# Scores of two heads as 64-row products on the halves of TensorE's array

## The chip, the cores and the metric

The kernel runs on one core of one Trainium2 chip. The metric is device time in microseconds (us) of one execution. Before the change the median of three runs is 859.24 us (858.61 to 861.03).

## What is computed

Attention with a block mask over 4 batches, 8 heads, 576 positions and head size 64, then two feed-forward layers over the 2304 tokens:

```python
scores = scale * np.matmul(q, k.transpose(0, 1, 3, 2))
mask = block_i >= block_j                 # blocks of 64 positions
scores = np.where(mask, scores, -1000000000.0)
attn = softmax(scores)
x = attn @ v                              # heads joined: 2304 x 512
h = np.maximum(np.maximum(x @ w1, x @ w2), x @ w3); y = h @ w_out
h = np.maximum(y @ w_in, 0.0);            out = h * h @ w_out2
```

Everything comes in as float32 (the feed-forward weights as 64-bit words). To keep that precision at speed, the kernel splits an operand into a rounded part ("hi", type fp32r) and what the rounding left ("lo"), and sums two or three fast products in place of one slow float32 product.

## The kernel before, in words

The work goes by **pairs** of heads: 16 pairs, four per batch. The first four pairs (n = 0 to 3, `S_F32` is 1) multiply float32 queries and keys directly; the other twelve (n = 4 to 15) use split operands made by `score_operands` (line 460 on). A pair has five steps, `step(0)` to `step(3)` with 128 queries each, and `last_step` with the 64 remaining queries of both heads side by side. Step i computes scores of 128 queries against N = 128(i+1) keys, head by head, into the PSUM banks `sc` (three buffers; steps 0 and 1 put both heads into one bank, as their widths fit). Then VectorE masks and takes the row maximum `nm`, ScalarE takes the exponential `P`, TensorE transposes `P` into `tp`, and after all steps `values` multiplies with the values into `av`. The value products use 64 columns of the array for each head; the last of them has only 64 rows as well.

For the scores of a split pair, `score_operands` loads for each head a tile `raw` in which queries and keys (64 features) stand twice, on partitions 0 to 63 and 64 to 127. The stationary tile `qs` holds the query's hi part in the upper half and its lo part in the lower, so that one 128-row product with the keys' hi part `kh` and one with the lo part `kl` give all four cross terms: two products a head. For `last_step` it loads keys and zero-padded queries once more (`kt`, `zt`) and splits them too (`k2`, `z2`).

While attention of batch b runs, the first feed-forward layer (`mlp1`) of an earlier batch fills TensorE: its products are called `l` in the profile. After attention (at about 375 us) come the rest of `mlp1` and then the second layer (`ph`, `acc`).

All compute instructions are recorded as operations and then issued by `Plan.issue`, which keeps a clock for each engine from the cost table in `duration` (line 316 on) and always issues the operation that could start first, the lower rank first among equals. So each engine's order is fixed in the program. Every operation is recorded at line 187. The engines and the DMA queue (SP) work through their lists in that order. TensorE's list alternates pieces of attention with `l` products.

Of the kernel before, what the change touches and what calls it, by code (L numbers as in the profile page):

```python
# [12 lines left out]
F32 = mybir.dt.float32  # L13
F32R = mybir.dt.float32r
I32 = mybir.dt.int32
U32 = mybir.dt.uint32
AF = mybir.ActivationFunctionType
ALU = mybir.AluOpType
# [5 lines left out]
B, H, S, D = 4, 8, 576, 64  # L24
# [13 lines left out]
TAIL = 512  # L38
# [3 lines left out]
SCALE = 0.125  # L42
PAIRS = B * NPAIR

CFG = dict(PD=-1, PE=1, A1=0, A2=0, WP=1, FC=(8, 16), WO=24, FI=0, LO2=0, HI2=0, Q2=0, RN=3, XL=2, HL=2, SO=0, TF=0, W_A=0.7, W_B=1.5, SPARE='hl..rhl..rhl..r..r..r', S=15, PB=3, QB=(2, 2, 3), BANKS=(3, 2, 1, 2), LO=0, HI=0, Q=0, EV=('*', '*'), EV2=('a', 'a'), CB=2, PC=0, PM=1000, PX=-0.5, PO=0, HH='*', XH='*', N0='a', YS='a', HIS=0, RB=1, TB=(2, 1), KB=1, CT='a', LT='d', XA=4, XB=0)
# [5 lines left out]
PB = CFG["PB"]  # L51
# [244 lines left out]
def width(x):  # L296
    return math.prod(x.area.shape[1:])
# [15 lines left out]
def duration(engine, op):  # L313
    views = op.views()
    n = max(map(width, views))
    psum = any(x.psum for x in views)
    if engine == "pe":
        stat, mov = op.args[1:] if op.args[1:] else (op.kw["lhsT"], op.kw["rhs"])
        if op.name == "transpose":
            return 109  # L320
        n, m = width(op.args[0]), width(stat)
        if stat.tile.args[1] == F32:
            return (4 * n / 2.4 + 5) * (0.5 if m == 64 else 1)
        return max(n, 230) / 2.4 + (11 if n < 300 else 13)
    if engine == "act":
        if op.name == "activation" and "accum_out" in op.kw:
            return 455 + 0.834 * n
        return (160 if psum else 200) + 0.82 * n
    if engine == "pool":
        return 140 + 2.25 * n  # L330
    if engine == "sp":
        return 60
    if op.name == "memset":
        return 60 + n
    if op.name == "reciprocal":
        return 150 + 6.4 * n
    if op.name in ("tensor_scalar", "tensor_copy", "copy") and not psum:
        return (200 if isinstance(op.kw.get("scalar1"), View) else 150) + n / 1.92
    return 157 + n / 0.96


def transfer(op):
    x = next(v for v in op.views())
    return 128 * 4 * width(x) / 320.0


@with_exitstack
def fused_kernel(ctx: ExitStack, tc: tile.TileContext, z0, k0, qk, v, w123, wo1, win2, wo2, out):
    nc = Plan(tc)
# [22 lines left out]
    def bank(name, tag):  # L372
        return ps.tile([128, 512], F32, tag=tag, bufs=BANKS[tag], name=name)
# [54 lines left out]
    def cp(e, **kw):  # L428
        return {"a": nc.scalar.copy, "d": nc.vector.tensor_copy, "*": nc.any.tensor_copy}[e](**kw)
# [22 lines left out]
    def small(name):  # L452
        return at.tile([128, 2], F32, tag=name[:2], bufs=6, name=name)
# [2 lines left out]

    def score_operands(n):


        score = []
        for h in range(2):
            raw = at.tile([128, 2, S], F32, tag="raw", bufs=CFG["RB"], name=f"raw{n}_{h}")
            nc.sync.dma_start(out=raw, in_=qk[n, :, h])
            qs, kh, kl = [at.tile([128, S], F32R, tag=t, bufs=m, name=f"{t}_{n}_{h}")
                          for t, m in zip(("qs", "kh", "kl"), CFG["QB"])]
            nc.scalar.activation(out=qs, in_=raw[:, 0], func=AF.Copy, scale=SCALE)
            nc.scalar.copy(out=kh, in_=raw[:, 1])
            nc.vector.scalar_tensor_tensor(out=qs[64:128], in0=raw[64:128, 0], scalar=SCALE,  # L470
                                           in1=qs[64:128].bitcast(F32), op0=ALU.mult, op1=ALU.subtract)
            nc.vector.tensor_tensor(out=kl, in0=raw[:, 1], in1=kh.bitcast(F32), op=ALU.subtract)
            score.append([(qs, kh), (qs, kl)])


        kt = at.tile([128, S], F32, tag="kraw", bufs=1 + CFG["TF"], name=f"kt{n}")
        zt = at.tile([128, 2, 64], F32, tag="zraw", bufs=1 + CFG["TF"], name=f"zt{n}")
        nc.sync.dma_start(out=kt, in_=k0[n])
        nc.sync.dma_start(out=zt, in_=z0[n, :, :, TAIL:])
        if CFG["TF"]:  # L480
            return score, [(zt.rearrange("p h q -> p (h q)"), kt)]
        k2 = [at.tile([128, S], F32R, tag=f"k2{x}", bufs=CFG["KB"], name=f"k2{x}_{n}") for x in "hl"]
        z2 = [at.tile([128, 2, 64], F32R, tag=f"z2{x}", bufs=CFG["KB"], name=f"z2{x}_{n}") for x in "hl"]
        for f, (hi, lo) in ((kt, k2), (zt, z2)):
            cp(CFG["CT"], out=hi, in_=f)
            (nc.gpsimd if CFG["LT"] == "p" else nc.vector).tensor_tensor(out=lo, in0=f, in1=hi.bitcast(F32), op=ALU.subtract)
        z2 = [z.rearrange("p h q -> p (h q)") for z in z2]
        return score, [(z2[1], k2[0]), (z2[0], k2[1]), (z2[0], k2[0])]

    def score_operands_f32(n, g):  # L490


        a, w = GROUPS[g] if n < NPAIR else (0, S)
        if n < NPAIR and g == 0:
            zk = at.tile([128, 3, GA], F32, tag="tb", bufs=2 * CFG["TB"][1], name=f"zk{n}")
            z, k = [zk[:, h] for h in range(2)], zk[:, 2]
        else:
            z = [at.tile([128, w], F32, tag=t, bufs=CFG["QB"][2 * (t == "kl")], name=f"z{n}_{t}") for t in ("qs", "kl")]
            k = at.tile([128, S], F32, tag="kh", bufs=CFG["QB"][1], name=f"k{n}")
        nc.sync.dma_start(out=z[0], in_=z0[n, :, 0, a:a + w])  # L500
        nc.sync.dma_start(out=k, in_=k0[n, :, :a + w])
        nc.sync.dma_start(out=z[1], in_=z0[n, :, 1, a:a + w])
        return [[(z[h], k)] for h in range(2)], None
# [25 lines left out]
    def attn_pair(n, groups=(0, 1)):  # L529
# [17 lines left out]
        def sc_tag(i):  # L547
            turn[0] += 1
            return "mlp" if (i < 2 and n < CFG["XA"] or i >= 2 and n < CFG["XB"]) and turn[0] % 5 in (1, 3) else "sc"
# [9 lines left out]
        def step(i):  # L559
# [1 line left out]
            name = f"{n}_{i}"  # L561

            share = i < 2
            sc = [bank(f"sc{name}_{h}", sc_tag(i)) for h in range(1 if share else 2)]
            P = [at.tile([128, 576], F32, tag="P", bufs=PB, name=f"P{name}_{h}") for h in range(len(sc))]
            if share:
                both = sc[0][:, :2 * N].rearrange("p (h k) -> p h k", h=2)
                sc = [both[:, h] for h in range(2)]
                P = [P[0][:, N * h:N * h + N] for h in range(2)]
            nm = small(f"nm{name}")  # L570
            scale = SCALE if sf else 1.0
            sm = sums[i // 2][:, 2 * (i % 2):2 * (i % 2) + 2] if direct else small(f"sm{name}")
            for h in range(2):
                for c, (qp, kp) in enumerate(score[h]):
                    mm(sc[h][:, :N], qp[:, 128 * i - q0:128 * i - q0 + 128], kp[:, :N], start=c == 0,
                       stop=c == len(score[h]) - 1)
                if not share:
                    nc.vector.memset(sc[h][0:64, N - 64:N], MASKED / scale)
                    nc.vector.tensor_reduce(out=nm[:, h:h + 1], in_=sc[h][:, :N], axis=AX.X, op=ALU.max, negate=True)
            if share:  # L580
                nc.vector.memset(both[0:64, :, N - 64:N], MASKED / scale)
                nc.vector.tensor_reduce(out=nm, in_=both, axis=AX.X, op=ALU.max, negate=True)
            if sf:
# [22 lines left out]
        def last_step():  # L606
# [3 lines left out]
            for x in range(2):  # L610
# [4 lines left out]
                else:  # L615
                    for c, (qp, kp) in enumerate(last):
                        mm(sc[x][:, :HALF], qp, kp[:, ks], start=c == 0, stop=c == len(last) - 1)
                nc.vector.tensor_reduce(out=nm[:, x:x + 1], in_=sc[x][:, :HALF], axis=AX.X, op=ALU.max, negate=True)
            nc.vector.tensor_scalar(out=nm[:, 0:1], in0=nm[:, 0:1], scalar1=nm[:, 1:2], scalar2=SCALE, op0=ALU.min,
                                    op1=ALU.mult)  # L620
            for x in range(2):
                act = nc.scalar.activation(out=P[:, HALF * x:HALF * x + HALF], in_=sc[x][:, :HALF], func=AF.Exp,
                                           bias=nm[:, 0:1], scale=SCALE, accum_out=sm[:, x:x + 1])
            nc.vector.tensor_scalar(out=sm[:, 0:1], in0=sm[:, 0:1], scalar1=sm[:, 1:2], scalar2=None, op0=ALU.add)
            if not direct:
                reciprocals(sm[:, 0:1])
# [40 lines left out]
                       ident[:, o:o + m], start=True, stop=True)  # L667
            return rows

        if 0 in groups:  # L670
            for i in range(2):
                step(i)
                yield
            values(0)
        if 1 in groups:
            for i in range(2, 4):
                step(i)
                yield
            last_step()
            yield  # L680
            values(1)

    def split_x(b, g):
        with nc.ranked(CFG["PX"]):
# [440 lines left out]
```

## Time and profile before

| what | value |
|---|---|
| median of three runs | 859.24 us |
| the profiled execution's own time | 860.5 us |
| its span, first to last instruction | 858.4 us |
| TensorE busy | 836.4 us, 97% of the span |
| VectorE busy | 641.3 us, 75% |
| ScalarE busy | 486.1 us, 57% |
| GpSimd busy | 131.0 us, 15% |
| moved by DMA | 190.32 MB |

The span is 2.1 us shorter than the execution's own time; the profiled execution is 1.3 us longer than the median. Matmuls are pipelined: a record of one lasts longer than the distance to the next one, so what a matmul costs TensorE is read from start to start in the timeline, not from its duration.

### The profile page before, as it was taken

The page shows a single profiled execution, that of the slowest core. Times are in us where ns is not written, and L with a number is a line of the kernel's source. Part 1 is how long each engine was busy: PE and PEld are TensorE (multiplying, and loading weights), DVE is VectorE, ACT ScalarE, POOL GpSimd, SP SyncE. Part 2 cuts the span into 40 slices and gives each one's busy share as a digit, 9 for nine tenths or more (in the row PEclk, how much of TensorE's full clock was granted, in tenths as well). Part 3 has the DMA queues.
Part 4 walks back from the last instruction along what each step waited for, and adds up shares of the span by engine and source line. Part 5 has one row for each costly group of instructions (what it writes and reads, how often), then busy time and mean ns, then how long its engine had stood idle before and what let it go on. Part 6 is the DMA issues. An engine that isn't in the chain of part 4 may idle for free.

```text
span 858.4 us, 15996 instructions
## 1 busy us (share of the span) xinstructions
PE 836.4 (97%) x5608; PEld 786.6 (92%) x5608; DVE 641.3 (75%) x1389; ACT 486.1 (57%) x1138; POOL 131.0 (15%) x126
## 2 busy tenths in 40 slices
PE   6899999999999999999999989999999999999998
PEld 4567799999899989999999989999999999999998
DVE  5998778888889888855667866688466876387663
ACT  6888778777787877756465332455232653133441
POOL 2334302122022011124445110000000000000000
PEclk9999999999999999999999999999999999999999
DMA  9554445465556446346787389898987878987782
GB/s 307 195 183 141 159 146 171 142 212 183 162 181 206 118 168 201 107 158 231 237 299 265 132 304 385 260 323 259 305 273 251 254 252 285 292 257 251 253 268 90
DMA packets 96575, 190.32 MB, mean 222 GB/s; under 512 B 13040, under 2 KB 23280, under 8 KB 96496
## 3 DMA queue, kind: packets, MB, share of 16 engines
q1 hardware_dynamic: 96496, 189.31, 66.4%
q8 instruction: 45, 0.74, 0.4%
q14 instruction: 34, 0.28, 0.1%
HBM read 150.47 MB, written 38.80 MB: 220 GB/s over the span
## 4 chain that ended last, share of the span: by engine, by line
PE 93%; DMA 3%; ACT 2%; DVE 2%; SPq 0%; issue 0%; ACTq 0%; DVEq 0%
PE l L187 35%; PE acc_x L187 12%; PE ph_x L187 11%; PE ph_z L187 8%; PE acc_z L187 6%; PE av L187 6%; PE sc L187 5%; PE tp L187 4%; PE acc_y L187 3%; PE sc_t L187 2%; DMA ws<-ws_d 1%; PE tp_t L187 1%; DMA raw<-in_qk 1%; DMA ws_d<-wst 1%; DMA zk<-in_k 1%; ACT P L187 0%
## 5 line engine op out<-in xcount | busy, mean ns | idle before, releaser
L187 PE MATMUL l<-xhl,w1h 128*128 128x320 f32 (+1 forms) x1152 | 244.8, 300 | 0.0
L187 PEld LDWEIGHTS l<-xhl,w1h 128*128 128x128 f32 x1152 | 188.4, 190 | 4.5 <-issue 2.9
L187 PE MATMUL l<-xhl,w1l 128*128 128x256 f32 (+1 forms) x576 | 175.0, 304 | 0.0
L187 PEld LDWEIGHTS l<-xhl,w1l 128*128 128x128 f32 x576 | 109.3, 190 | 3.4 <-issue 1.5
L187 PE MATMUL acc_x<-g_p,ws 128*128 128x384 f32 x576 | 102.2, 335 | 0.0
L187 PEld LDWEIGHTS acc_x<-g_p,ws 128*128 128x128 f32 x576 | 100.1, 188 | 0.0
L187 PE MATMUL l<-hh,wo 128*128 128x320 f32 (+1 forms) x384 | 81.6, 298 | 2.9 <-DVE wo L187 2.1
L187 PE MATMUL ph_x<-t,ws 128*128 128x384 f32 x432 | 80.8, 335 | 0.0
L187 PEld LDWEIGHTS ph_x<-t,ws 128*128 128x128 f32 x432 | 75.4, 188 | 0.0
L187 ACT ACTIVATE P<-sc,nm 128x128 f32<-128x128 f32 (+3 forms) x128 | 66.8, 532 | 9.5 <-DVE nm L187 7.0
L187 DVE TENSOR_TENSOR run<-l,run 128x256 f32<-128x256 f32 (+1 forms) x96 | 43.7, 455 | 32.2 <-PE l L187 30.6
L187 PEld LDWEIGHTS l<-hh,wo 128*128 128x128 f32 x384 | 63.3, 190 | 3.7 <-DVE wo L187 2.5
L187 ACT CAST g_p<-c_wo 128x768 fp32r<-128x768 f32 x42 | 35.1, 836 | 38.7 <-PE acc_x L187 15.7
L187 PE MATMUL l<-hl,wo 128*128 128x256 f32 (+1 forms) x192 | 57.0, 299 | 0.0
L187 PE MATMUL tp<-ident,P 128*128 128x128 f32 x320 | 52.9, 281 | 4.2 <-ACT P L187 3.9
L187 PE MATMUL ph_z<-b,ws 128*128 128x384 f32 x288 | 53.9, 336 | 2.9 <-DMA ws<-ws_d 2.9
L187 DVE TENSOR_TENSOR g_p<-c_wo,g_p 128x768 fp32r<-128x768 f32 x42 | 39.9, 955 | 22.0 <-ACT g_p L187 21.8
L187 DVE TENSOR_REDUCE nm<-sc 128x2 f32<-128x256 f32 (+2 forms) x96 | 54.6, 588 | 0.6
L187 POOL TENSOR_TENSOR f_wo<-f_wo,raw_wo 128x512 int32<-128x512 int32 x22 | 30.3, 1378 | 161.6 <-ACT t L187 34.7
L187 PEld LDWEIGHTS ph_z<-b,ws 128*128 128x128 f32 x288 | 50.2, 188 | 3.2 <-issue 3.2
L187 PE MATMUL acc_z<-g_p,ws 128*128 128x384 f32 x288 | 51.2, 335 | 0.0
L187 PEld LDWEIGHTS acc_z<-g_p,ws 128*128 128x128 f32 x288 | 50.1, 188 | 0.0
(168 smaller groups left out, 1653.1 us busy)
## 6 DMA issues: line engine op xcount, KB each, us to landing
ws<-ws_d SPq DMA_DIRECT2D x336, 256.0 KB, 3.9
ws_d<-wst SPq DMA_DIRECT2D x64, 256.0 KB, 3.4
raw<-in_qk SPq DMA_DIRECT2D x24, 576.0 KB, 3.8
ws_d<-wst SPq DMA_DIRECT2D x24, 512.0 KB, 5.9
raw_wo<-in_wo SPq DMA_DIRECT2D x22, 512.0 KB, 3.8
raw_w<-in_w SPq DMA_DIRECT2D x18, 512.0 KB, 5.0
raw_wi<-in_win SPq DMA_DIRECT2D x16, 512.0 KB, 5.2
v<-in_v SPq DMA_DIRECT2D x16, 320.0 KB, 3.4
```

Source lines behind the costliest of these rows:

```text
L187: return getattr(engine, op_name)(*map(value, args), **{k: value(x) for k, x in kw.items()})
```

## The change

Queries and keys are loaded once per pair, head 0 on partitions 0 to 63 and head 1 on 64 to 127, and rounded once: one tile `parts` with query hi, key hi, key lo, query lo. A score step makes three products a head, lo x hi, hi x lo and hi x hi, each of 64 rows: head 0 on the upper half of TensorE's rows, head 1 on the lower, each head into a bank of its own. The products alternate between the heads, and the first of each two is recorded as waiting for what the second waits for. `last_step` uses the same `parts` for the keys, and queries copied into a zero-padded tile `z2`, which is cleared once at the start. The copies `kt`, `zt`, `k2` are gone. Steps 0 and 1 of split pairs now mask and reduce each head apart. The float32 pairs keep their way of working (their tiles have moved into the tag `parts`). `duration` gets a cost for the new products, and so the written order changes on all engines.

```diff
@@ duration
+        if m == 128 and stat.area.shape[0] == 64:
+            return (4 * n if stat.tile.args[1] == F32 else max(n, 230)) / 4.8 + 6
@@ score_operands
+        raw = at.tile([128, 2, S], F32, tag="raw", bufs=CFG["RB"], name=f"raw{n}")
+        nc.sync.dma_start(out=raw, in_=qk[n])
+        parts = at.tile([128, 4, S], F32R, tag="parts", bufs=2, name=f"parts{n}")
+        qh, kh, kl, ql = [parts[:, i] for i in range(4)]
+        nc.scalar.copy(out=kh, in_=raw[:, 1])
+        nc.scalar.activation(out=qh, in_=raw[:, 0], func=AF.Copy, scale=SCALE)
+        nc.vector.tensor_tensor(out=kl, in0=raw[:, 1], in1=kh.bitcast(F32), op=ALU.subtract)
+        nc.vector.scalar_tensor_tensor(out=ql, in0=raw[:, 0], scalar=SCALE, in1=qh.bitcast(F32), op0=ALU.mult,
+                                       op1=ALU.subtract)
+        z = z2[n % 2]
         score = []
         for h in range(2):
-            raw = at.tile([128, 2, S], F32, tag="raw", bufs=CFG["RB"], name=f"raw{n}_{h}")
...
-            score.append([(qs, kh), (qs, kl)])
...
+            rows = slice(64 * h, 64 * h + 64)
+            score.append([(x[rows], y[rows]) for x, y in ((ql, kh), (qh, kl), (qh, kh))])
+            nc.vector.tensor_copy(out=z[rows, :, 64 * h:64 * h + 64], in_=parts[rows, 0:4:3, TAIL:])
+        return score, [(z[:, 1], kh), (z[:, 0], kl), (z[:, 0], kh)]
@@ step
+            if rows:
+                for c in range(len(score[0])):
+                    pair = [product(h, c) for h in range(2)]
+                    pair[0].deps |= pair[1].deps
```

**TensorE, step 0 of pair 7** (`sc` is the score bank, `l` a feed-forward product; `x2` counts equal rows, the last size is that of the output). Before, head 0's two products, with feed-forward products before and after:

```order
582 L187 MATMUL l_0_1_5_0_2201<-xhl_1_647,w1l_990 128x320
583 L187 MATMUL sc_0_0_2222<-kh_0_2099,qs_0_2144 128x128
584 L187 MATMUL sc_0_0_2222<-kl_0_2121,qs_0_2144 128x128
585 L187 MATMUL l_0_1_5_0_2201<-xhl_1_647,w1h_951 128x320 x2
586 L187 MATMUL l_0_1_5_0_2201<-xhl_1_647,w1l_990 128x320
```

Now, both heads' products in one stretch of six, again between feed-forward products:

```order
598 L187 MATMUL l_0_1_5_1_2210<-xhl_1_630,w1h_915 128x320 x2
599 L187 MATMUL sc_0_0_2225<-parts_1895 128x128
600 L187 MATMUL sc_0_1_2227<-parts_1895 128x128
601 L187 MATMUL sc_0_0_2225<-parts_1895 128x128
602 L187 MATMUL sc_0_1_2227<-parts_1895 128x128
603 L187 MATMUL sc_0_0_2225<-parts_1895 128x128
604 L187 MATMUL sc_0_1_2227<-parts_1895 128x128
605 L187 MATMUL l_0_1_5_1_2210<-xhl_1_630,w1l_937 128x320
```

A step's four products of 128 rows (sixteen a pair in its four steps) have become six of 64 rows (twenty-four a pair), and the six stand together between products of 128 rows.

**TensorE, step 3 of pair 7.** Before, the products of 512 keys:

```order
657 L187 MATMUL sc_3_0_2433<-kh_0_2099,qs_0_2144 128x512
658 L187 MATMUL tp_0_0_2438<-ident,P_0_0_2380 128x128 x2
659 L187 MATMUL sc_3_0_2433<-kl_0_2121,qs_0_2144 128x512
660 L187 MATMUL l_0_1_1_2388<-hh_1_1607,wo_1107 128x320
661 L187 MATMUL sc_3_1_2449<-kh_1_2291,qs_1_2269 128x512
662 L187 MATMUL sc_3_1_2449<-kl_1_2341,qs_1_2269 128x512
```

Now, behind value products (64 columns) and ahead of the last step (128 rows):

```order
683 L187 MATMUL av_0_2468<-ta_2420,v_0_2026 64x128 x2
684 L187 MATMUL sc_3_0_2474<-parts_1895 128x512
685 L187 MATMUL sc_3_1_2478<-parts_1895 128x512
686 L187 MATMUL sc_3_0_2474<-parts_1895 128x512
687 L187 MATMUL sc_3_1_2478<-parts_1895 128x512
688 L187 MATMUL sc_3_0_2474<-parts_1895 128x512
689 L187 MATMUL sc_3_1_2478<-parts_1895 128x512
690 L187 MATMUL sc_t_2488<-parts_1895,z_116 128x288 x3
```

Here one side of the stretch meets value products, so that only one of its borders is new against products of 128 rows and columns.

**ScalarE, the operands of pair 7.** Before, with other work between them, five long roundings (`qs`, `kh` for either head, `k2h`) and a short one (`z2h`), of which four rows stand here:

```order
255 L187 ACTIVATE qs_0_2144<-raw_0_1988 128x576
256 L187 COPY xf_2155<-av_0_2135 128x256
257 L187 ACTIVATE f_wo_2160<-raw_wo_1704 128x512
258 L187 CAST k2h_2171<-kt_1918 128x576
```

Now two, together:

```order
225 L187 CAST parts_1895<-raw_1594 128x576
226 L187 ACTIVATE parts_1895<-raw_1594 128x576
```

They stand some thirty rows earlier in ScalarE's list than before.

## Rows read from the trace of the kernel before

**Rows 1.** The page: span, busy time of each engine, TensorE's busy tenths.

```profile
span 858.4 us, 15996 instructions
...
PE 836.4 (97%) x5608; PEld 786.6 (92%) x5608; DVE 641.3 (75%) x1389; ACT 486.1 (57%) x1138; POOL 131.0 (15%) x126
...
PE   6899999999999999999999989999999999999998
```

**Rows 2.** Windows: stretch and length; busy PE, PEld, DVE, ACT, POOL; PE clock, DMA share, GB/s.

```profile
100.00:120.00 20.00, 17.47 (x138) 15.12 (x138) 15.12 (x39) 12.10 (x32) 2.41 (x2) 1.00 0.32 104
...
200.00:220.00 20.00, 20.00 (x165) 19.37 (x163) 18.58 (x54) 13.77 (x40) 4.79 (x5) 1.00 0.49 160
```

**Rows 3.** Waits of PE, 95 to 125 us: total us, times, longest.

```profile
PE l L187 <- DVE wo L187: 2.1, 2, 1.7
PE l L187 <- ACT ys L187: 0.8, 1, 0.8
```

**Rows 4.** Timeline of PE, about 200 us: start, us from first start to last end, operation.

```profile
201.33 0.34 PE L187 MATMUL sc<-kh,qs 128*128 128x384 f32 x1
201.51 0.34 PE L187 MATMUL sc<-kl,qs 128*128 128x384 f32 x1
...
203.00 0.28 PE L187 MATMUL l<-xhl,w1l 128*128 128x256 f32 x1
203.12 0.28 PE L187 MATMUL l<-xhl,w1h 128*128 128x256 f32 x1
...
204.28 0.39 PE L187 MATMUL sc<-kh,qs 128*128 128x512 f32 x1
204.51 0.40 PE L187 MATMUL sc<-kl,qs 128*128 128x512 f32 x1
```

**Rows 5.** Timeline of PE, about 110 us: two score products of 128 keys.

```profile
110.29 0.39 PE L187 MATMUL sc<-kh,qs 128*128 128x128 f32 x2
110.52 0.40 PE L187 MATMUL l<-hh,wo 128*128 128x256 f32 x2
```

**Rows 6.** Timeline of PE, 153.0 to 156.4 us: from feed-forward over value products to scores.

```profile
153.01 0.31 PE L187 MATMUL l<-xhl,w1h 128*128 128x320 f32 x1
153.16 0.31 PE L187 MATMUL l<-xhl,w1l 128*128 128x320 f32 x1
153.40 2.16 PE L187 MATMUL av<-tb,v 128*64 128x320 f32 x16
155.49 0.33 PE L187 MATMUL av<-t,v 64*64 64x64 f32 x4
155.75 0.44 PE L187 MATMUL sc<-kh,qs 128*128 128x384 f32 x1
156.03 0.34 PE L187 MATMUL sc<-kl,qs 128*128 128x384 f32 x1
```

**Rows 7.** Timeline of PE, window from 155.3 us: the last four of those sixteen.

```profile
155.06 0.49 PE L187 MATMUL av<-tb,v 128*64 128x192 f32 x4
```

**Rows 8.** Timeline of PEld, the weight loads, same place.

```profile
155.75 0.19 PEld L187 LDWEIGHTS sc<-kh,qs 128*128 128x128 f32 x1
155.86 0.19 PEld L187 LDWEIGHTS sc<-kl,qs 128*128 128x128 f32 x1
```

**Rows 9.** Lines by form: count | busy us, mean ns | idle before.

```profile
L187 PE MATMUL l<-xhl,w1h 128*128 128x320 f32 x576 | 133.4, 313 | 0.0
...
L187 PE MATMUL av<-tb,v 128*64 128x320 f32 x192 | 30.5, 441 | 0.0
...
L187 ACT ACTIVATE qs<-raw 128x576 fp32r<-128x576 f32 x24 | 16.5, 688 | 5.0 <-DMA raw<-in_qk 4.3 <-PE sc L187 0.7
...
L187 PE MATMUL sc<-kh,qs 128*128 128x512 f32 x24 | 10.0, 415 | 0.0
...
L187 DVE TENSOR_TENSOR k2l<-kt,k2h 128x576 fp32r<-128x576 f32 x12 | 9.0, 750 | 0.1
...
L187 ACT CAST k2h<-kt 128x576 fp32r<-128x576 f32 x12 | 8.2, 685 | 2.8 <-PE sc_t L187 2.7
```

More of the change, by code (lines that the diff above doesn't have):

```diff
@@ L343, in transfer @@
     x = next(v for v in op.views())
-    return 128 * 4 * width(x) / 320.0
+    return 4 * math.prod(x.area.shape) / 320.0
 @with_exitstack
@@ L453, in small @@
         return at.tile([128, 2], F32, tag=name[:2], bufs=6, name=name)
+    z2 = [at.tile([128, 2, 128], F32R, tag=f"z2{i}", name=f"z2{i}") for i in range(2)]
+    for z in z2:
+        nc.gpsimd.memset(z.bitcast(F32), 0.0)
     def score_operands(n):
+        raw = at.tile([128, 2, S], F32, tag="raw", bufs=CFG["RB"], name=f"raw{n}")
[8 more added lines that the diff above has]
+        z = z2[n % 2]
@@ L462, in score_operands @@
         score = []
         for h in range(2):
-            raw = at.tile([128, 2, S], F32, tag="raw", bufs=CFG["RB"], name=f"raw{n}_{h}")
[L465 to L471, printed above, removed]
@@ L472, in score_operands @@
-            nc.vector.tensor_tensor(out=kl, in0=raw[:, 1], in1=kh.bitcast(F32), op=ALU.subtract)
-            score.append([(qs, kh), (qs, kl)])
[L476 to L488, printed above, removed]
+            rows = slice(64 * h, 64 * h + 64)
@@ L497, in score_operands_f32 @@
         else:
-            z = [at.tile([128, w], F32, tag=t, bufs=CFG["QB"][2 * (t == "kl")], name=f"z{n}_{t}") for t in ("qs", "kl")]
-            k = at.tile([128, S], F32, tag="kh", bufs=CFG["QB"][1], name=f"k{n}")
+            zk = at.tile([128, 3, S], F32, tag="parts", bufs=2, name=f"zk{n}_{g}")
+            z, k = [zk[:, h, :w] for h in range(2)], zk[:, 2]
         nc.sync.dma_start(out=z[0], in_=z0[n, :, 0, a:a + w])
@@ L563, in step @@
             share = i < 2
-            sc = [bank(f"sc{name}_{h}", sc_tag(i)) for h in range(1 if share else 2)]
-            P = [at.tile([128, 576], F32, tag="P", bufs=PB, name=f"P{name}_{h}") for h in range(len(sc))]
+            rows = not sf
+            sc = [bank(f"sc{name}_{h}", sc_tag(i)) for h in range(2 if rows or not share else 1)]
+            P = [at.tile([128, 576], F32, tag="P", bufs=PB, name=f"P{name}_{h}") for h in range(1 if share else 2)]
             if share:
+                P = [P[0][:, N * h:N * h + N] for h in range(2)]
+            if len(sc) == 1:
                 both = sc[0][:, :2 * N].rearrange("p (h k) -> p h k", h=2)
                 sc = [both[:, h] for h in range(2)]
-                P = [P[0][:, N * h:N * h + N] for h in range(2)]
+            else:
+                both = None
             nm = small(f"nm{name}")
@@ L572, in step, with product @@
             sm = sums[i // 2][:, 2 * (i % 2):2 * (i % 2) + 2] if direct else small(f"sm{name}")
+            def product(h, c):
+                qp, kp = score[h][c]
+                return mm(sc[h][:, :N], qp[:, 128 * i - q0:128 * i - q0 + 128], kp[:, :N], start=c == 0,
+                          stop=c == len(score[h]) - 1)
+            if rows:
+                for c in range(len(score[0])):
+                    pair = [product(h, c) for h in range(2)]
+                    pair[0].deps |= pair[1].deps
             for h in range(2):
[L574 to L577, printed above, removed]
+                if not rows:
+                    for c in range(len(score[h])):
+                        product(h, c)
+                if both is None:
                     nc.vector.memset(sc[h][0:64, N - 64:N], MASKED / scale)
                     nc.vector.tensor_reduce(out=nm[:, h:h + 1], in_=sc[h][:, :N], axis=AX.X, op=ALU.max, negate=True)
-            if share:
+            if both is not None:
                 nc.vector.memset(both[0:64, :, N - 64:N], MASKED / scale)
@@ L618, in last_step @@
                 nc.vector.tensor_reduce(out=nm[:, x:x + 1], in_=sc[x][:, :HALF], axis=AX.X, op=ALU.max, negate=True)
-            nc.vector.tensor_scalar(out=nm[:, 0:1], in0=nm[:, 0:1], scalar1=nm[:, 1:2], scalar2=SCALE, op0=ALU.min,
+            scale = SCALE if sf else 1.0
+            nc.vector.tensor_scalar(out=nm[:, 0:1], in0=nm[:, 0:1], scalar1=nm[:, 1:2], scalar2=scale, op0=ALU.min,
                                     op1=ALU.mult)
@@ L622, in last_step @@
                 act = nc.scalar.activation(out=P[:, HALF * x:HALF * x + HALF], in_=sc[x][:, :HALF], func=AF.Exp,
-                                           bias=nm[:, 0:1], scale=SCALE, accum_out=sm[:, x:x + 1])
+                                           bias=nm[:, 0:1], scale=scale, accum_out=sm[:, x:x + 1])
             nc.vector.tensor_scalar(out=sm[:, 0:1], in0=sm[:, 0:1], scalar1=sm[:, 1:2], scalar2=None, op0=ALU.add)
@@ L668, in sum_rows, with first @@
             return rows
-        if 0 in groups:
+        def first():
             for i in range(2):
@@ L674, in attn_pair, with second @@
             values(0)
-        if 1 in groups:
-            for i in range(2, 4):
-                step(i)
+        def second():
+            steps = [lambda: step(2), lambda: step(3)]
+            steps.append(last_step)
+            for f in steps:
+                f()
                 yield
-            last_step()
-            yield
             values(1)
+        for f in (first, second):
+            if (0 if f is first else 1) in groups:
+                yield from f()
     def split_x(b, g):
@@ L1097 @@
     z0, k0 = z0.reshape(PAIRS, 128, 2, S), kn.reshape(PAIRS, 128, S)
-    qk = np.stack([a.transpose(0, 2, 1, 3) for a in (qn, kn)], axis=3)
-    qk = np.concatenate([qk, qk], axis=1)
+    qk = np.stack([a.reshape(PAIRS, 128, S) for a in (qn, kn)], axis=2)
     vr = v.reshape(PAIRS, 2, S, D).transpose(0, 2, 1, 3)
```

## The prediction, made before the changed kernel ran

> **What bounds the kernel now.** I read the page first. TensorE is busy 97% of the span, and in its tenths nothing but the first two slices and one or two later ones is below 9 [rows 1]. Busy time alone says little for pipelined matmuls, so the windows come next: about 200 us, in the middle of attention, TensorE has no idle time at all in 20 us, while VectorE has 1.4 us left and ScalarE 6.2 us [rows 2]. The only stretch of attention with split operands in which TensorE idles for over 2 us is that from 100 to 120 us, 2.53 us [rows 2], and the table of waits gives the cause: `l` products that wait for feed-forward weights (`wo`) out of VectorE and for a bank that ScalarE empties, 2.9 us [rows 3]. So between about 103 us (the first split score) and the end of attention a microsecond of TensorE is a microsecond of the kernel, and what ScalarE, VectorE and DMA save is hidden under it. The sum is therefore made of what the change costs and saves in TensorE's own list.
>
> **A score product, from start to start.** Two products of 128 keys and the start of what follows are 0.23 us apart, so 0.115 each [rows 5]; 256 columns take 0.12 (a feed-forward product of the same width), 384 take 0.18, 512 take 0.23 [rows 4]. One product of each width is 0.645 us together. Before, a step makes four (two heads, two products): 4 x 0.645 = 2.58 us a pair. Now it makes three places of two products side by side, if both halves of the array work at once: 3 x 0.645 = 1.94. That saves 0.645 us a pair, and with 12 split pairs **7.7 us**. The trace has no product on half of the rows and all columns. It has two heads side by side on column halves: 192 value products of 441 ns in 30.5 us busy, 2.8 deep, where 576 feed-forward products of 313 ns fill 133.4 us, 1.35 deep [rows 9]. So side by side works for columns, and I take it for rows.
>
> **A change of shape.** What has to be weighed against this is seen where the value products begin and end [rows 6]. Feed-forward products of 320 columns start 0.15 us apart, so the one at 153.16 leaves TensorE at 153.31; the value products start at 153.40, 0.09 late. The sixteen of them hold six places of 320 columns and two of 192; the places of 320 take from 153.40 to 155.06 [rows 6, 7], 1.66 us. If about 0.05 of that is the first weight load, a place is 0.27 us, or 0.84 ns a column; the two places of 192 columns should take 0.32 us and take 0.43, till the 64-row products start at 155.49 [rows 6, 7]. That is 0.1 us lost where **only the number of rows changes**, 128 to 64. These four fill two places of 64 columns, 0.11 us, and the score behind them starts 0.26 later: 0.05 for a first load and again 0.10 lost. Then the first score product holds TensorE for 0.28 us instead of 0.18, 0.10 more; the weight loads show why: the second load starts 0.11 us after the first [rows 8], and behind a change of shape the first load has no product to hide under. So a change into a shape with 128 columns costs 0.10 + 0.105 = **0.205 us**, into one with 64 columns 0.09 + 0.05 = 0.14. The new shape, 64 rows by 128 columns, has 128 columns of weights; its two loads go to different rows and I let them run at once. Its nearest row is the change of rows at 155.49, with the load of 128 columns at 155.75.
>
> The Trainium skill has this as a rule: TensorEngine Tiling (Array Packing), section Tiling Modes, says that changing the tiling mode, not just the tile, drains TensorE. The lost 0.1 us at each border agrees; how much load comes on top the page doesn't say.
>
> **How many changes.** I counted the shapes along the whole written order, with the narrow transpose `tq` as a full one. Before there are 104 changes: 46 into 128x64, 42 back into 128x128, 16 into 64x64. Now there are 200: 44, 85, 16, and 55 into the new 64x128. A pair has four stretches of six products; most are whole, seven are cut by the order, and some borders meet value products and were there anyway. The sum: 55 x 0.205 + 43 x 0.205 - 2 x 0.14 = **19.8 us**. Bounds for the price of one: below 0 (a split by rows might not count as a change of shape), above 0.205 with some margin; I take 0.205, as the row for a change of rows alone [rows 6, 7] shows the loss.
>
> **The rest, on other engines.** ScalarE loses three of five roundings of 576 columns a pair, 0.69 us each [rows 9], 25 us over 12 pairs, and the short `z2h`; VectorE loses three of five passes of about 0.75 us [rows 9], 27 us, less two short copies, one more mask and one more reduce in each of steps 0 and 1. DMA moves 576 KB a pair instead of 1,504 KB. All this lies beside TensorE, which is full; if that cover were gone, it would be a gain, never a loss. The two cleared `z2` tiles stand in GpSimd's list ahead of its first weights; GpSimd is busy 15% of the span [rows 1]. Steps 0 and 1 now take two of three `sc` banks each, so scores start less far ahead; the feed-forward products between them cover that, at nothing. The one place where lighter engines can tell is the wait of 2.9 us between 95 and 125 us [rows 3], where roundings of queries and keys stand between the weights. It can go or stay; I take half, **-1.5 us**.
>
> **The sum.** -7.7 + 19.8 - 1.5 = +10.6 us on the profiled execution's 860.5 us: 871.1. That execution is 1.3 us above the median, so **869.8 us** for the median, 1.2% slower. If a change of shape costs as little as 0.08 us (7.7 over 96 more changes), TensorE is even; from there on the change loses.
>
> **Rivals.** First, *free borders*: half rows at full columns are no change of shape, and weights load under the product before. Then only the saving is left: 859.2 - 7.7 - 1.5 = 850.0, faster. It decides below 0.08 us a border. For it speaks that no row shows this shape; against it the 0.1 us where rows alone change [rows 6, 7]. Chance 0.10. The Trainium skill's TensorE: Matmul & The Clock Gate (Part 3) has weight loads overlap running products where the row group differs; by that rule alone this rival would come near, and no row here shows it.
> Second, *half-price borders*: the loss of 0.095 but a hidden load: 96 x 0.095 = 9.1, and 859.2 - 7.7 + 9.1 - 1.5 = 859.1, no change. Against it stands the 0.28 us of the first score [rows 6]. Chance 0.11.
> Third, *the halves don't work side by side*, so that the change doesn't do what it says. If the two loads follow each other, 0.11 us each [rows 8], a place takes 0.23 us at every width: twelve places a pair are 2.76 us where there were 2.58, and 12 x 0.18 = 2.1 us are lost instead of 7.7 saved, 879.6. Chance 0.09. If the products too follow each other, six products of each width cost 1.29 us a pair more than four, 15.5 instead of -7.7, and 893. Against both: the value products' depth [rows 9]. Chance 0.05.
>
> **How the numbers follow.** The forecast has the remaining 0.65; its own range is 863 to 876, from borders at 0.15 us with the whole wait gone (859.2 - 7.7 + 14.4 - 2.9 = 863.0) to 0.22 and a wait that grows as much as it was hoped to shrink (859.2 - 7.7 + 21.1 + 1.5 = 874.1, and two for places cut by the order). The range from 857 to 880 takes in the half-price case and the loads one after the other, and leaves out the two ends, 0.15. About 0.3%, 2.6 us, can be told from no change here: faster 0.11, the same 0.11, slower 0.78.
>
> **What would show it.** In the profile after: two score records of 64 rows that start within some 10 ns of each other, the next two one width later; a gap of 0.09 to 0.10 us ahead of each stretch of six and behind it, and a first place about 0.1 us too long on either side; attention's end some 10 to 12 us later; ScalarE some 25 us and VectorE some 20 us less busy; TensorE as full as now. The prediction is wrong if stretches border on feed-forward products without a gap, if a pair of records doesn't start together, or if TensorE shows new waits for `nm`, `P` or a bank between 120 us and attention's end.

## The result and the profile after

The changed kernel takes 864.06 us (median of five, 862.77 to 867.52), the kernel before 859.48 us over five runs. The ratio is 1.0054 with a 95% interval of 1.0029 to 1.0079: **4.6 us slower**, where 10.6 us slower was forecast. The sign and the time's range held; the size is less than half.

The profiled execution is the slowest of the five (867.52 us). TensorE's granted clock is 0.91 between 520 and 540 us in it and 1.00 in every window of 20 us from 40 us up to there, so what lies behind 520 us is not compared. The page's first lines:

```profile
span 865.7 us, 16011 instructions
...
PE 847.5 (98%) x5704; PEld 782.6 (90%) x5704; DVE 619.8 (72%) x1417; ACT 463.8 (54%) x1086; POOL 129.1 (15%) x128
...
PE   6899999999999999999999999999999999999998
```

Against [rows 1], VectorE is 21.5 us less busy, ScalarE 22.3 us, and TensorE's tenths have no 8 between the second slice and the last. The windows for [rows 2], and one of those in between:

```profile
100.00:120.00 20.00, 19.34 (x157) 16.49 (x154) 15.81 (x52) 13.35 (x39) 1.60 (x1) 1.00 0.46 155
200.00:220.00 20.00, 20.00 (x169) 17.82 (x165) 16.93 (x61) 14.43 (x44) 2.80 (x4) 1.00 0.36 125
220.00:240.00 20.00, 20.00 (x165) 17.19 (x164) 15.36 (x54) 13.36 (x37) 4.83 (x5) 1.00 0.40 136
```

From 100 to 120 us TensorE idles 0.66 us instead of 2.53. In the window from 220 to 240 us it idled 1.03 us before and now doesn't idle at all. This is the row of the window before, and with it the product ahead of which TensorE idled, waiting for ScalarE:

```profile
220.00:240.00 20.00, 18.97 (x154) 16.86 (x154) 16.68 (x52) 16.33 (x48) 3.41 (x3) 1.00 0.49 162
```

```profile
221.26 0.66 PE L187 MATMUL tp_t<-ident,P_t 128*128 128x128 f32 x4 [1.03 <-ACT tb L187]
```

The table of waits for [rows 3], 95 to 125 us, is down to one row:

```profile
PE l L187 <- DVE wo L187: 0.7, 1, 0.7
```

Now the stretches of 64-row products, in TensorE's timeline. First one of 128 keys, then one of 256, then one of 512:

```profile
143.03 0.46 PE L187 MATMUL l<-xhl,w1h 128*128 128x320 f32 x2
143.42 0.55 PE L187 MATMUL sc<-parts 64*128 64x128 f32 x6
143.90 0.42 PE L187 MATMUL l<-xhl,w1l 128*128 128x320 f32 x1
144.15 0.32 PE L187 MATMUL l<-xhl,w1h 128*128 128x320 f32 x1
...
147.63 0.31 PE L187 MATMUL l<-xhl,w1l 128*128 128x320 f32 x1
147.87 0.62 PE L187 MATMUL sc<-parts 64*128 64x256 f32 x6
148.42 0.56 PE L187 MATMUL l<-xhl,w1h 128*128 128x320 f32 x2
148.82 0.31 PE L187 MATMUL l<-xhl,w1l 128*128 128x320 f32 x1
...
132.49 0.46 PE L187 MATMUL l<-xhl,w1h 128*128 128x320 f32 x2
132.87 0.99 PE L187 MATMUL sc<-parts 64*128 64x512 f32 x6
133.79 0.41 PE L187 MATMUL l<-xhl,w1l 128*128 128x320 f32 x1
134.04 0.42 PE L187 MATMUL sc_t<-parts,z 128*128 128x288 f32 x2
```

In the middle one, the product at 147.63 leaves TensorE at 147.78 (0.15 a product of 320 columns, as in [rows 6]); the stretch starts at 147.87, 0.09 late; the two feed-forward products behind it take from 148.42 to 148.82, 0.40 where 0.30 is usual. So it holds TensorE from 147.78 to 148.52, 0.74 us, for three places of two products side by side (3 x 0.12 = 0.36): **0.38 us for two borders**. Four full products of 256 columns, as before, were 0.48. At 512 keys the stretch holds it from 132.79 to 133.89, 1.10 us, for 0.92 before [rows 4]; at 128 keys from 143.33 to 144.00, 0.67 for 0.46 [rows 5].

Read in the same way, the whole stretches of the changed kernel that stand between full products take 0.67 us at 128 keys (median of 12), 0.75 at 256 (of 9), 0.92 at 384 (of 9) and 1.09 at 512 (of 7), for 0.46, 0.48, 0.72 and 0.92 us before. So no width gains, and the two borders of a stretch cost 0.33, 0.39, 0.38 and 0.40 us, **on average 0.19 us a border**.

That the two halves work at once shows in the widest: six products of 512 columns one after another would take 6 x 0.23 = 1.38 us, and the next product starts 0.92 us after the first of them. The weight loads run two at a time as well, which the prediction had assumed. Here are the six of the stretch of 256 keys; one after another, 0.11 us apart as in [rows 8], they would last over 0.7 us:

```profile
147.87 0.42 PEld L187 LDWEIGHTS sc<-parts 64*128 64x128 f32 x6 [0.19 <-issue]
```

### The profile page after: what moved, and what is told of

Its sections match the earlier page's. It is cut to its first block, busy times and chain, and to the rows that moved or that the text cites. A ratio compares the mean times of both kernels' runs of the same rounds, so it can differ in the third digit from the quotient of the medians.

```text
span 865.7 us, 16011 instructions
## 1 busy us (share of the span) xinstructions
PE 847.5 (98%) x5704; PEld 782.6 (90%) x5704; DVE 619.8 (72%) x1417; ACT 463.8 (54%) x1086; POOL 129.1 (15%) x128
## 4 chain that ended last, share of the span: by engine, by line
PE 94%; ACT 2%; DMA 2%; DVE 2%; SPq 0%; issue 0%; DVEq 0%; ACTq 0%
PE l L187 36%; PE acc_x L187 12%; PE ph_x L187 11%; PE ph_z L187 8%; PE acc_z L187 6%; PE av L187 6%; PE sc L187 5%; PE tp L187 4%; PE acc_y L187 3%; PE sc_t L187 2%; DMA ws<-ws_d 1%; PE tp_t L187 1%; DMA zk<-in_k 1%; ACT P L187 0%; PE r L187 0%; DVE f_w L187 0%
## 5 line engine op out<-in xcount | busy, mean ns | idle before, releaser
L187 DVE TENSOR_REDUCE nm<-sc 128x1 f32<-128x384 f32 (+4 forms) x120 | 58.6, 502 | 0.4
L187 PEld LDWEIGHTS tp<-ident,P 128*128 128x128 f32 x320 | 38.1, 143 | 13.7 <-ACT P L187 6.1
```

The lines of the kernel that those rows point to most:

```text
L187: return getattr(engine, op_name)(*map(value, args), **{k: value(x) for k, x in kw.items()})
```

## Experiments

All are timed against the kernel before on the same chip; its median was 859.2 to 860.1 us there. Times of the changed kernel are its own 864.06 us.

**One more shape inside each stretch (border).**

```diff
                     pair[0].deps |= pair[1].deps
+                    if c == 0:
+                        mm(sc[1][:, :128], zero, full_keys[n][:, :128], start=False, stop=False)
```

> The changed kernel with one more product behind the first two of each score step of a split pair: 128 rows, a stationary tile of zeros, 128 columns, added to head 1's bank (it adds zero). 48 such products, each cutting a stretch of 64-row products in two. My theory, that a change of shape costs TensorE about 0.19 us (0.09 late start plus 0.10 of first weight load) wherever it stands: 104 more changes in the written order, 19.6 us, plus 48 x 0.11 = 5.4 us for the products: 25 us slower than the changed kernel, about 889 us. Rival, half-price borders (only the gap of 0.09, the load hidden): 104 x 0.09 + 5.4 = 15 us, about 879. Rival, free borders, the slowdown has another cause (banks, reduces): 5.4 us, about 869.5.

Measured: 889.55 us, ratio 1.0343 (1.0318 to 1.0368), 25.5 us above the changed kernel: the border theory's number. Less 5.4 us for the products, 104 changes of shape cost 20.1 us, **0.19 us each**. The profiled executions say a little less: from the first split score to the second layer it is 428.1 us (101.26 to 529.40) against 404.8, which leaves 17.9 us, 0.17 each. In its timeline, a stretch of 384 keys:

```profile
130.54 0.44 PE L187 MATMUL sc<-parts 64*128 64x384 f32 x2
130.92 0.33 PE L187 MATMUL sc<-parts,zero 128*128 128x128 f32 x1
131.17 0.62 PE L187 MATMUL sc<-parts 64*128 64x384 f32 x4
131.72 0.42 PE L187 MATMUL l<-xhl,w1l 128*128 128x320 f32 x1
```

Two products side by side, 0.18 us wide, are followed 0.38 us later by the added one. The 0.20 us between fit the prediction's two parts, 0.10 for the first load and 0.10 for the change behind it. Half-price borders (0.09 us each) and free ones are out by either figure.

**The preparation put back, the planner told (prep_back).**

```diff
+        again = at.tile([128, 2, S], F32, tag="raw", bufs=CFG["RB"], name=f"raw{n}_again")
+        nc.sync.dma_start(out=again, in_=qk[n])
...
+        for f, w in ((again[:, 0], 512), (again[:, 1], 512), (kt, 512), (zt, 128)):
...
+            nc.scalar.copy(out=hi[:, :w], in_=f[:, :w])
+            nc.vector.tensor_tensor(out=f[:, :w], in0=f[:, :w], in1=hi[:, :w].bitcast(F32), op=ALU.subtract)
```

> The changed kernel with the removed preparation put back as work nobody reads: a second load of queries and keys and one of the zero-padded ones for each split pair, three roundings and subtractions of 512 columns and one of 128 on ScalarE and VectorE (576 before). If lighter ScalarE and VectorE removed the waits of about 4 us that TensorE had between the first split score and the second layer, the waits come back: 3 to 5 us slower than the changed kernel, 867 to 869 us (its order has 8 more stretches of 64-row products, 1.7 us of that). If the waits went by the new order alone: only the 1.7 us, about 865.5.

Measured: 881.50 us, ratio 1.0250 (1.0231 to 1.0269), 17.4 us above the changed kernel, far over either expectation. Two of its waits of TensorE:

```profile
PE ph_x L187 <- DMA ws<-ws_d: 8.3, 1, 8.3
...
PE sc L187 <- DVE parts L187: 1.6, 1, 1.6
```

About half of it is one wait of 8.3 us at the start of the second layer (`ph_x`), for weights that ScalarE, VectorE and GpSimd split and write to memory. The order moved with the load, so this run can't tell the one from the other.

**Order alone (plan_only).** The kernel before, the planner's cost of split scores cut to 0.75:

```diff
-        return max(n, 230) / 2.4 + (11 if n < 300 else 13)
+        return (max(n, 230) / 2.4 + (11 if n < 300 else 13)) * (0.75 if op.args[0].tile.tag == "sc" and n != HALF else 1)
```

> The kernel before with one number changed: the planner takes a split score product at three quarters of its cost, so that the written order moves and the work stays the same. It tells how far order alone moves the time. If the waits of 4 us between 100 and 225 us hang on the order: anything from 856 to 861 us, with the waits for feed-forward weights at 105 us gone or grown. If they hang on the load of ScalarE and VectorE: within 1 us of the kernel before, the waits still there.

Measured: 873.11 us, ratio 1.0149 (1.0131 to 1.0168), 13 us slower with the same work, outside both expectations. The timeline shows where:

```profile
500.55 0.31 PE L187 MATMUL l<-hh,wo 128*128 128x320 f32 x1
516.52 1.33 PE L187 MATMUL ph_x<-b,ws 128*128 128x384 f32 x3 [15.66 <-DMA ws<-ws_d]
```

TensorE ends the first layer at 500.55 us, 1.3 us sooner than before (501.89), and then waits 15.66 us for second-layer weights. Before, it waits 2.9 us for such weights some 13 us into that layer, and in the changed kernel 2.4. The waits at 105 us (2.6 us) are still there, but that of 1.0 us at 221 us is gone, by the order alone. So the written order decides over far more than this change is worth, and a run whose order moves is read by its waits, not by its time.

**The load put back with every list in the changed kernel's order (load_back).** Behind the last rounding of each pair three more run on either engine; the planner doesn't know of them:

```diff
+        last_act.behind = [("copy", dict(out=extra[0], in_=raw[:, 1, :512]))] * 3
+        last_dve.behind = [("tensor_tensor", dict(out=extra[1], in0=raw[:, 1, :512], in1=kh[:, :512].bitcast(F32), op=ALU.subtract))] * 3
```

> The changed kernel, every list in the same order, with three more roundings of 512 columns put behind the rounding of the queries on ScalarE and three more subtractions of 512 columns behind that on VectorE, for each split pair; nobody reads them, and the planner isn't told. So the load that the change took away is back (about 2.0 us an engine and pair) and the order is that of the change. If the lighter engines removed TensorE's waits: 3 to 4 us slower than the changed kernel, 867 to 868 us. If the new order removed them: within 1 us of it, 863.5 to 865.5.

Measured: 874.37 us, ratio 1.0175 (1.0151 to 1.0198), **10.3 us above the changed kernel**. The added work by the groups of lines, and two windows with those of the changed kernel behind them:

```profile
L188 DVE TENSOR_TENSOR extra<-raw,parts 128x512 fp32r<-128x512 f32 x36 | 26.0, 721 | 0.8
L188 ACT CAST extra<-raw 128x512 fp32r<-128x512 f32 x36 | 22.3, 620 | 0.8
...
100.00:120.00 20.00, 16.68 (x120) 13.96 (x117) 17.00 (x47) 12.41 (x35) 1.61 (x1) 0.91 0.39 131
120.00:160.00 40.00, 39.15 (x286) 32.74 (x285) 34.09 (x112) 29.99 (x82) 5.59 (x6) 1.00 0.37 124
```

```profile
120.00:160.00 40.00, 40.00 (x293) 32.90 (x291) 31.96 (x109) 26.38 (x75) 6.90 (x7) 1.00 0.37 119
```

TensorE idles 3.32 us from 100 to 120 us (0.66 in the changed kernel) and 0.85 in the next 40 us (none there). The long wait, 3.2 us for `wo`, is for a pass of VectorE that stands close behind three of the added ones in its list (their first took 1.8 us, the others 0.7; why is open):

```profile
100.36 3.26 DVE L188 TENSOR_TENSOR extra<-raw,parts 128x512 fp32r<-128x512 f32 x3
...
105.12 0.67 DVE L188 TENSOR_TENSOR wo<-f_wo,wo 128x512 fp32r<-128x512 f32 x1
```

From the first split score to the second layer the trace has 414.6 us (101.63 to 516.22), 9.8 more than the changed kernel. TensorE's idle rows are 6.0 us of that part, where they were 0.7. The clock of 0.91 in the first window, 1.00 in the changed kernel, is worth at most 1.8 us (0.09 of 20 us). Some 2.7 us or more stand in no row. So the roundings that the change removed were not free under a full TensorE: in this order, some 22 to 26 us of them on each engine cost 10 us, a part of it through the clock. The added passes stand three in a row and also hold `raw`, which has one buffer, for longer; what they would cost in other places was not run.

**Part of the load removed in the order of before (ghost_last).** The work for the last step is planned but not issued:

```diff
+            if not op.ghost:
                 self.tc.keep_in_program_order(self.call(self.real[e], alias(e, op.name), op.args, op.kw))
```

> The kernel before, every list in the same order, without the loads, roundings and subtractions for the last step (kt, zt, k2, z2) from the second split pair on: the planner still counts them, but they are not issued, and the last step of these pairs multiplies the first split pair's tiles, so that its results are not attention's. TensorE's list is that of before to the last row; ScalarE and VectorE lose about 1.0 us each a pair. If lighter engines remove TensorE's waits: 2 to 3 us faster than before, 857 to 858 us. If the order alone sets them: within 1 us of before, 859 to 860.5.

Measured: 857.75 us, ratio 0.9991 (0.9971 to 1.0011). The median lies where lighter engines would put it, but the interval goes from 2.5 us faster to 0.9 slower, so the time tells no difference. The trace tells one. Between 95 and 500 us, these are all waits in the table:

```profile
PE l L188 <- DVE wo L188: 1.7, 2, 1.3
PE l L188 <- ACT ys L188: 0.2, 1, 0.2
```

That is 1.9 us instead of 3.9 ([rows 3], and the 1.0 us at 221 us), with every list in the order of before and some 9 us less work on each engine. So lighter engines alone did take waits away, in this execution. What it gained shows only in part, as its clock fell where that of before did not [rows 2]:

```profile
100.00:120.00 20.00, 18.19 (x131) 16.15 (x131) 14.26 (x39) 12.27 (x33) 2.79 (x2) 0.91 0.31 106
```

From the first split score to the second layer it has 397.6 us (103.67 to 501.29), 1.1 less than before. Together with load_back: at an order that was written for the heavy load, some 9 us less on each engine are worth 2.5 us at the most, by the interval; at an order that was written for the light load, 22 to 26 us more cost 10.

**Two tries to lighten the kernel before (no_last_prep, last_f32).** The first lets the last step use the other tiles in place of its own load and split, the second turns one number, `TF=0` to `TF=1`.

```diff
-        return score, [(z2[1], k2[0]), (z2[0], k2[1]), (z2[0], k2[0])]
+        return score, [(q1_[:, 448:], k0_), (q0_[:, 448:], l0_), (q0_[:, 448:], k1_)]
```

> The kernel before without the second load and split of keys and of padded queries for the last step: that step multiplies other tiles of the same shape, so TensorE's products, shapes and borders are those of before, and ScalarE and VectorE lose about 1.0 us each a pair; its results in the last 64 rows are not attention's. Theory, that lighter ScalarE and VectorE take away TensorE's waits: of the about 4.9 us between the first split score and the second layer 2 to 3.5 go, 856 to 857.5 us. Rival, that the waits depend on the order alone: no change of the sum of waits, 859 to 860, or a jump from the wait for second-layer weights.

> The kernel before with the last step of split pairs as one float32 product instead of three split ones, straight from what is loaded: TensorE has 24 products of about 0.48 us for 72 of 0.133, 2 us more, ScalarE and VectorE lose about 1.0 us each a pair. If lighter engines give back 2 to 3.5 us of waits: 857.5 to 859.5 us. If they give nothing: 861.5.

Measured: 874.05 us, ratio 1.0165 (1.0138 to 1.0191), and 866.57 us, ratio 1.0085 (1.0061 to 1.0110). Both miss. The first is a poor experiment: its last step holds `qs`, `kh` and `kl` of head 0 until the pair's end, and two or three buffers don't seem to last (between 95 and 500 us, TensorE waits 2.4 us for `qs` at one place and 5.4 us for `P` at five). In the second the order moved again (2.9 us for `wo`). Neither tells anything of the load by itself.

**Fewer borders (merge01_inf, whole, whole_cost).** Steps 0 and 1 share one bank per head, and their products stand in one stretch of twelve. This is the edit of whole and whole_cost, which keeps a stretch uncut; merge01_inf records the twelve together and leaves it to a planner that knows of borders not to cut them:

```diff
+            if rows and i != 1:
+                made = []
+                for k, dest in ((0, sc), (1, first_banks)) if i == 0 else ((i, sc),):
+                    made += [product(h, c, k, dest) for c in range(len(score[0])) for h in range(2)]
+                for op in made[1:]:
+                    made[0].deps |= op.deps - set(made)
+                    op.rank = -1
```

> The changed kernel with steps 0 and 1 of a split pair in one bank per head (128 and 256 columns), their twelve products recorded together, and a planner that is told of 190 ns for each change of shape and prefers, once in a shape, to stay there for up to 200 ns. The written order has 36 stretches of 64-row products after the first one instead of 55, and 30 fewer changes of shape. Border theory: 5.9 us faster than the changed kernel, about 858 us, level with the kernel before or up to 0.2% faster. Rival, the slowdown comes from something other than borders: no faster than 863 us.

> The changed kernel with steps 0 and 1 of a split pair in one bank per head, and the products of a stretch (twelve of steps 0 and 1, six of step 2, six of step 3) never cut by others. 36 stretches behind the first split score instead of 55, and 33 fewer changes of shape; the planner is not told of borders. Border theory, at 0.19 us a change of shape: 6.4 us less on TensorE than in the changed kernel, about 857.7 us if the waits stay as small as there, level with or just under the kernel before. Rival, that the written order elsewhere decides (waits for P and nm, and the wait for second-layer weights): 860 to 875 with TensorE's waits grown by what is missing.

> The kernel with uncut stretches and steps 0 and 1 together (36 stretches) once more, with a planner that takes each 64-row product 44 ns dearer, nearer to what a stretch costs with its borders. Work and number of borders are the same within one or two; only the order differs. Border theory with waits as small as in the changed kernel: 857 to 858 us. If the order brings other waits: 859 to 870.

Measured: merge01_inf 865.95 us, ratio 1.0065 (1.0050 to 1.0080); whole **861.01 us, ratio 1.0013 (0.9997 to 1.0029)**, level with the kernel before; whole_cost 864.87 us, ratio 1.0060 (1.0040 to 1.0080). All three have 30 to 33 fewer changes of shape than the changed kernel, some 6 us of TensorE by the price above; only whole shows half of that (3.1 us by the medians, and as much from the first split score to the second layer, 401.8 us for 404.8). The waits take a part of the rest: between 95 and 500 us the table has 2.5 us of them in whole and 3.7 us each in whole_cost and merge01_inf (the changed kernel 0.7). The longest of whole_cost, for score banks at six places, then two of merge01_inf, in that stretch:

```profile
PE sc L187 <- DVE sc L187: 1.8, 6, 0.4
```

```profile
PE sc_t L188 <- ACT P L188: 1.3, 2, 1.1
PE sc L188 <- DVE sc L188: 0.7, 3, 0.2
```

Waits shorter than 0.2 us each are not in the tables; how much of what is missing lies in them was not followed up, so that fewer borders give back time is shown by whole alone.

## Why the prediction was right and wrong

**Bound and mechanism: right.** TensorE's list sets the time through attention, the two halves of the array work at once, and every stretch pays at both ends. By rows, from the first split score to the first product of the second layer it was 103.36 to 502.04 us, 398.7 us, before, and is 102.92 to 507.75, 404.8 us, after (the first two rows before, the others after):

```profile
103.36 0.67 PE L187 MATMUL sc<-kh,qs 128*128 128x128 f32 x3
...
502.04 1.25 PE L187 MATMUL ph_x<-b,ws 128*128 128x384 f32 x6
```

```profile
102.92 0.55 PE L187 MATMUL sc<-parts 64*128 64x128 f32 x6
...
507.75 1.03 PE L187 MATMUL ph_x<-b,ws 128*128 128x384 f32 x5
```

6.1 us more, where the two terms -7.7 and +19.8 said 12.1.

**The saving, -7.7 us: right**, by the widths that the stretches show. **The borders, +19.8 us: close, about 2 us too dear.** In the part between those rows, TensorE's list has 7.7 us less of scores and nine feed-forward products of 0.12 us less (2060 for 2069), 1.1 us. Its idle rows are 3.6 us before (1.72 and 0.81 of [rows 3], the rest of which lies ahead of this part, and the 1.03 us at 221 us) and 0.7 us after, 2.9 us less. So 6.1 + 7.7 + 1.1 + 2.9 = 17.8 us are left for 99 more changes of shape in this part (159 for 60), 0.18 us each. That lies between the 0.17 and the 0.19 of border; the forecast had 0.205. Waits too short for a row, if more or fewer of them went, would move it.

**The wait at 100 to 120 us, -1.5 us: the step that failed.** It was the only place where I let lighter engines tell, and I took half of 2.9 us. Of the 3.6 us of idle rows behind the first split score nearly all went (0.7 left), among them the 1.03 us at 221 us, whose window I had read and not priced. Ahead of the first split score another 1.5 us went: the new list does the nine feed-forward products there, 1.1 us, and still that score comes 0.4 us sooner. So waits and order gave 4.4 us where 1.5 were forecast, and the borders, taken as what is left, cost 17.8 where 19.8 were. Less these 2.9 and 2.0 us, the forecast 10.6 is the 5.7 us by which the second layer starts later (507.75 against 502.04). The medians say 4.6. Single executions differ by as much: in the five traces that have the same number of products ahead of the first split score (the changed kernel, border, load_back, whole, whole_cost) it starts between 100.03 and 102.92 us, so the 1.5 us ahead of it is the least certain of these terms.

**"All this lies beside TensorE, which is full; if that cover were gone, it would be a gain, never a loss": wrong in its first half.** A full TensorE was no cover: ScalarE and VectorE feed it in lists of fixed order. At the same order, load_back shows 10 us for load that comes back, and ghost_last 2.0 us of waits that go with load that is taken away. The order moves waits too: in plan_only the one at 221 us went without any change of load. How the waits that the change took away divide between lighter engines and the new order stays open.

Of the rivals, free and half-price borders fall with border, the halves one after another with the stretch rows and the row of their weight loads. What the prediction names in favour of free borders, weight loads that overlap where the row group differs, does not speak for them: the product ahead of a stretch works on all 128 rows, and the first loads of the stretch above start with its first products, at 147.87 us. The savings of ScalarE and VectorE (forecast 25 and some 20 us, measured 22.3 and 21.5) were right. No run of the whole computation beats the kernel before; whole is level with it, at 36 stretches. At 0.19 us a border a stretch must save more than 0.38 us, and at the widest single step it saves 0.23 us.

## What to carry to other kernels

Products on half of the array's rows, which here took three places where there were four, pay only if enough of them stand together: price each stretch with two changes of shape before counting what runs side by side. Where lists have a fixed order, an engine that is 60 to 85% busy (the two in load_back's windows) still sets waits of the full one, so give work taken off it a price of its own, with a bound from a run that puts the load back in the same order. Time a reordering by itself first; here one planner number moved the time nearly three times as far as the change.

## What was not expected of the hardware

A change of rows alone, at 128 columns, costs 0.17 to 0.19 us, as the mean of in and out, measured over 104 of them in border. TensorE's clock was granted at 0.91 from 100 to 120 us in load_back, with 3.3 us idle in that window, and in ghost_last, with 1.8 us idle, but at 1.00 in the kernel before, with 2.5 us idle. So the idle time of that window does not by itself say whether the clock falls, and two traces of nearly the same list can differ by it.
